# Attention and token mixing on one core: value products in three pieces, a plan that counts instructions, and the queries' factor on another engine

## The chip, the cores and the metric

One NeuronCore of a Trainium2 chip. It has TensorE (matmuls, PE), VectorE (DVE), ScalarE (ACT), GpSimd (POOL) and SyncE (SP, which issues transfers here), each with a queue of its own that runs in order. The time is that of one execution on the device, in microseconds (us); lower is better.

## The reference

Thresholded attention over 8 batches x 8 heads, 576 rows, head size 64, and behind it a mixing layer over 512 channels, all in float32:

```
scores = (q @ k.T) / 8
attn = softmax over the scores >= max(scores) - tau, others 0
x = attn @ v                       # heads side by side: 576 x 512 for each batch
theta = x @ w_theta
y = w_tok_r @ (x * cos(theta)) + w_tok_i @ (x * sin(theta))
u = x + y
out = u + relu(u @ w_ch)
```

## The kernel before

Two heads make a pair; there are 32 pairs, four to a batch. A float32 factor is split into a high and a low part of a faster type (`q1, q2`, `k1, k2`, `xh, xl`, `zh, zl`, `wt_h, wt_l`), and a product is the sum of three products of parts.

A pair's attention is five *units* of 128 rows (`unit`, four with two heads, the last with the rest of both). For each: 12 or 6 score matmuls into banks 0 to 3 of PSUM (L572); a VectorE pass from PSUM with the factor -1/8 that also gives the row minimum (L587, factor in `gate`, a column of `small`); the exponential on ScalarE (L612); mask, multiply and row sum on VectorE (L619). The factor's sign follows tau's, and the maximum becomes a minimum by it.

The weights then have to be turned, keys onto partitions, into the tile `a`, of which there is one. Most pairs are turned by VectorE in blocks of 32 x 32 (L634, L636); for pairs 0 to 5 and every fourth one after, `BY_PE` is true and TensorE turns them (L652), with copies by ScalarE (L658, L670). The value product follows: for pairs turned by TensorE with 64 rows (L711), for the others with 32 rows and 64 columns (L688), `products` inside `values`, 18 groups of keys in one go into four banks (0 to 3) at once. Float32 matmuls are run in two passes each, so that 144 matmuls of the code are 288 in the trace. ScalarE copies the result into `xT` (L695, L698), and `divide` multiplies by the inverse row sums, turned by L739, stored and spread by transfers, on GpSimd or VectorE (L762).

The mixture of batch b (L814 for both channel products, L935 turns, L964 the token product) runs beside the attention of batch b + 1; the last one runs alone. At the start the weights w_theta and w_tok are split (`convert`) beside the first pairs.

The order on every engine is made ahead of time by a planner in the kernel. Every operation is given an engine, a duration, a key, what it reads and writes and the buffers it needs. `run` simulates the engines: of the operations that can begin about now it takes the one with the lowest key, for TensorE with an addition for a change of form (`SWITCH` in time, `favour` in the key). The order that comes out is the program; on the chip, semaphores alone decide when something begins. Keys are in units of which a pair has 9; the offsets and shares are the numbers of `AT`. Buffers more than one bank wide (scores and the L688 product) take banks 0 to 3 in the order of the code, which has the product of pair n - 1 behind units 0 and 1 of pair n (`vq`).

Of the kernel before, what the change touches and what calls it, by code (L numbers as in the profile page):

```python
# [28 lines left out]
PE, DVE, ACT, POOL, SP = range(5)  # L29

SEM = 0.06
TABLE = 1.29
AT = {
    "wait": 0.06, "margin": 0.0, "held": 1.155, "theta": 2.75, "theta_by": 2.91, "tok": 8.25, "tok_by": 4.06, "ch": 32.56,
    "ch_by": 6.81, "q": -4.55, "k": -10.96, "raw": -2.84, "v": -0.24, "m0": 8.14, "m1": 4.71, "score": -3.28, "nm": -0.39,
    "add": -2.31, "exp": -2.15, "mask": 0.59, "wrap": -0.41, "turn": 1.01, "copy": 2.31, "block": 0.3, "turn_by": 0.3,
    "last": 0.68, "v0": 6.08, "v1": 15.08, "vcopy": 7.63, "div": 3.45, "rows": -1.17, "dmul": -1.49, "x": -0.85, "x_by": 0.29,
    "wm": -8.18, "ev": 4.38, "zst": 1.58, "sin": 1.57, "zm": 2.24, "zh": 1.93, "zl": -4.81, "y": -5.29, "u": 1.65, "fa": -0.31,
    "fa_by": 1.34, "ft": 0.17, "ft_by": 0.15, "pq": 29, "px": 2, "pu": 1, "pz": 7, "pk": 1, "ta": 4, "cut": 2, "pp": 0,
    "vm": 0, "m6": -0.56, "wp": 0, "wq": 0, "ua": 4, "ord": 0, "hang": 0, "n_rawq": 2, "n_rawk": 1, "n_q": 4, "n_rb": 2,  # L40
    "n_ang": 2, "n_xh": 4, "n_xl": 4, "n_wm": 3, "n_z": 3, "n_k": 4, "n_s2": 3, "n_nm": 4, "n_sc": 4, "n_a": 1, "n_zh4": 4,
    "n_zl4": 4, "n_zh1": 2, "n_zl1": 2, "n_xT": 7, "n_v": 1, "n_rows": 2, "n_rt": 1, "keep": -1.73, "linger": 0.03,
    "v_r": -0.13, "v_m": 0.0, "t_s": -0.57, "m_s": 1.63, "wc": 14, "early": 6, "each": 1, "ka": 4, "vq": 1, "pd": 4,
# [67 lines left out]
class Op:  # L111

    def __init__(self, n, eng, occ, tail, fn, key, lock, mode):
        self.n, self.eng, self.occ, self.lat, self.fn, self.key = n, eng, occ, occ + tail, fn, key
        self.lock, self.mode = lock, mode
        self.deps, self.after, self.bufs = {}, [], []
        self.start, self.left, self.ready, self.kb, self.then = None, 0, 0.0, 0.0, None


class Plan:  # L120
# [4 lines left out]
    def op(self, eng, occ, fn, key, R=(), W=(), tail=0.07, lock=False, mode=None, hold=()):  # L125
        o = Op(len(self.ops), eng, occ, tail, fn, key, lock, mode)
        o.hold = hold

        def need(d, full):
            if d is not o:  # L130
                o.deps[d] = o.deps.get(d, False) or full

        for x in R:
            b, parts = x if isinstance(x, tuple) else (x, list(x.writers))
            for p in parts if isinstance(parts, list) else [parts]:
                for d in b.writers.get(p, ()):
                    need(d, True)
                if b.psum:
                    for d in b.readers.get(p, ()):
                        need(d, d.eng != eng)  # L140
                b.readers.setdefault(p, []).append(o)
            if b not in o.bufs:
                o.bufs.append(b)
        for x in W:
            b, parts = x if isinstance(x, tuple) else (x, 0)
            for p in parts if isinstance(parts, list) else [parts]:
                for d in b.writers.get(p, []) + b.readers.get(p, []):
                    need(d, d.eng != eng)
                b.writers[p], b.readers[p] = [o], []
            if b not in o.bufs:  # L150
                o.bufs.append(b)
        for b in o.bufs:
            b.left += 1
        for d in o.deps:
            d.after.append(o)
        o.left = len(o.deps)
        self.ops.append(o)
        return o

    def run(self):  # L160
# [9 lines left out]

        def begin(o):
            t = max(free[o.eng], o.ready)
            taken = {}
# [49 lines left out]
        while todo:  # L223
# [48 lines left out]
def tile_attn_moe(  # L272
# [89 lines left out]
    def c_pool(n):  # L362
        return n * 0.0024 + 0.066

    def pe(occ, fn, key, R, W, mode="m", hold=()):
        return op(PE, occ, fn, key, R, W, tail={"m": 0.21, "t": 0.22, "v": 0.28, "w": 0.28, "r": 0.28}[mode], mode=mode, hold=hold)
# [30 lines left out]
    def convert(src, n, raw_cls, places, key, done, turn):  # L397
# [34 lines left out]
        if turn < AT["wc"]:  # L432
            for i in range(2):
                gps(
                    c_pool(n // 2), lambda i=i: clamp(nc.gpsimd, slice(n * i // 2, n * (i + 1) // 2)), key, ((mag, i),),
                    ((mag, i),),
                )
        else:
            dve(c_fast(n), lambda: clamp(nc.vector), key, (mag,), ((mag, [0, 1]),), lock=True)
# [33 lines left out]
        for c in range(0, n, n2):  # L473
# [9 lines left out]
            pe(0.485 * n2 / 288 + 2 * c_mm(n2), sum_up, key, (bits, w, hi_b), (ps,))  # L483
# [40 lines left out]
    def prepare_q(n, key):  # L524
# [3 lines left out]
        q1, q2 = pr.q = [sb("q", [P, QS], F32R) for _ in range(2)]  # L528
        act(c_act(QS), lambda: nc.scalar.copy(out=q1(), in_=raw()), key, (raw,), (q1,))  # L529
# [25 lines left out]
    def unit(n, i):  # L555
# [11 lines left out]
        def score():  # L567
# [11 lines left out]
            mode="r" if i < 4 else "m",  # L579
# [3 lines left out]
        for j in heads:  # L583
            sc = scs[j] = sb("sc", [P, S])
            dve(
                c_ps(S) + 0.008,
                lambda j=j, sc=sc: nc.vector.tensor_scalar(  # L587
                    out=sc().rearrange("p (a b) -> p a b", a=2), in0=ps()[:, 2 * j : 2 * j + 2, :HS], scalar1=gate, scalar2=None,
# [6 lines left out]
            0.1,  # L595
# [32 lines left out]
        if not pe_way:  # L628
            for j in heads:
# [8 lines left out]
                dve(c_two(S), blocks, t0 + j + AT["block"], ((s, j),), ((a, (i, j)),), lock=True)  # L638
# [6 lines left out]
        for x, (c0, nb) in enumerate(runs):  # L645
# [8 lines left out]
            pe(0.109 * nb, turn_round, t0 + AT["turn"] + AT["turn_by"] * x, ((s, list(heads)),), (tp,), mode="t", hold=(a,))  # L654
# [8 lines left out]
            else:  # L663
# [10 lines left out]
                act(2 * halves * c_act(nb * 64, True), lay, t0 + AT["copy"] + AT["turn_by"] * x, (tp,), ((a, (i, x)),))  # L674

    def values(n, key):
        pr, x = pairs[n], xT[n]
        a, v = pr.a, pr.v
        if not BY_PE(n):
# [3 lines left out]
            def products():  # L683
                for c in range(18):
# [7 lines left out]
            pe(18 * w / 600 + 0.05, products, key, (a, v), (ps,), mode="w", hold=[x])  # L692
# [22 lines left out]
        pe(9 * w / 600 + 0.05, products, key, (a, v), outs, mode="v", hold=[x])  # L715
# [10 lines left out]
    def divide(n, key):  # L726
# [13 lines left out]
            mode="t", hold=(rt,),  # L740
        )
        act(c_act(P, True), lambda: nc.scalar.copy(out=rt(), in_=tp()[:9, :P]), key + AT["rows"], (tp,), (rt,))
# [38 lines left out]
    def mixture(b, k0, k1):  # L781
# [11 lines left out]
        def product(which, m, parts, last_chunk, evict, hold=()):  # L793
# [10 lines left out]
            for run in runs:  # L804
                for q in range(0, len(run), 4 if len(run) % 4 == 0 else 3):
# [6 lines left out]
                    def go(piece=piece, h=h, first=first, final=final):  # L812
# [9 lines left out]
                        (ps[h],), hold=hold,  # L822
# [4 lines left out]
        def angle(m):  # L827
# [42 lines left out]
            )  # L870
            dve(
# [53 lines left out]
        def flip(m, keys):  # L925
            z = zs[m]
            out = []
            for (c0, nb), key in zip(((0, 4), (4, 1), (5, 4)), keys):
# [11 lines left out]
                pe(0.109 * nb, turn, key, ((z, zp(0) if c0 == 0 else zp(0, 1) if c0 == 4 else zp(1)),), (tp,), mode="t", hold=(zh, zl))  # L940
# [11 lines left out]
        def token(m):  # L952
            zz = zs[m, "T"]
            for h in range(2):
# [4 lines left out]
                for q in range(0, len(work), 3):  # L959
# [13 lines left out]
                    pe(3 * c_mm(HS), go, now(0.393), (*need.values(), *ws), (ps,))  # L973
# [153 lines left out]
```

## Time and profile before

| | us |
|---|---|
| three runs | 998.86, 999.94, 1008.34 |
| median | 999.94 |
| profiled execution, its time | 997.56 |
| its span in the profile | 995.8 |

The profile is one execution; its busy times, waits and timelines are read against its own 997.56 us. A line such as `L688` is a line of the kernel before. PE are matmuls and PEld the weight loads that overlap them.

### The profile page before, as it was taken

The page shows a single profiled execution, that of the slowest core. Times are in us where ns is not written, and L with a number is a line of the kernel's source. Part 1 is how long each engine was busy: PE and PEld are TensorE (multiplying, and loading weights), DVE is VectorE, ACT ScalarE, POOL GpSimd, SP SyncE. Part 2 cuts the span into 40 slices and gives each one's busy share as a digit, 9 for nine tenths or more (in the row PEclk, how much of TensorE's full clock was granted, in tenths as well). Part 3 has the DMA queues.
Part 4 walks back from the last instruction along what each step waited for, and adds up shares of the span by engine and source line. Part 5 has one row for each costly group of instructions (what it writes and reads, how often), then busy time and mean ns, then how long its engine had stood idle before and what let it go on. Part 6 is the DMA issues. An engine that isn't in the chain of part 4 may idle for free.

```text
span 995.8 us, 29743 instructions
## 1 busy us (share of the span) xinstructions
PE 917.0 (92%) x12357; PEld 808.2 (81%) x12357; DVE 822.6 (83%) x1963; ACT 606.6 (61%) x1154; POOL 337.8 (34%) x380
## 2 busy tenths in 40 slices
PE   6888899999899998999999998999999998998998
PEld 4565687888798877888888887898788887988898
DVE  7999968879799796997989797997979797986352
ACT  6888888546673556646675566646565466724550
POOL 4466354213351233512354143512344133500200
PEclk9999999999999999999999999999999999999999
DMA  6673234425433464225633365135633354222502
GB/s 229 196 209 110 62 125 132 145 82 167 154 82 80 124 192 111 68 58 161 183 83 75 97 185 169 46 81 150 182 85 84 96 155 142 59 51 74 176 19 69
DMA packets 59863, 118.21 MB, mean 119 GB/s; under 512 B 20272, under 2 KB 29008, under 8 KB 57296
## 3 DMA queue, kind: packets, MB, share of 16 engines
q1 hardware_dynamic: 59728, 116.31, 40.3%
q8 instruction: 97, 1.59, 0.7%
q14 instruction: 38, 0.31, 0.1%
HBM read 102.50 MB, written 13.78 MB: 117 GB/s over the span
## 4 chain that ended last, share of the span: by engine, by line
PE 52%; DVE 26%; issue 8%; ACT 7%; POOL 5%; DMA 1%; SPq 0%; DVEq 0%; POOLq 0%; ACTq 0%
PE banks_ps__66 L964 18%; PE banks_ps__66 L688 10%; PE banks_ps__66 L814 9%; DVE s L619 8%; DVE sc L587 8%; PE banks_ps__66 L572 8%; DVE a L634 3%; PE banks_ps__66 L935 3%; PE banks_ps__66 L652 2%; POOL z L910 2%; ACT s L612 2%; PE banks_ps__66 L711 1%; POOL q L385 1%; POOL xl L385 1%; ACT a L670 1%
## 5 line engine op out<-in xcount | busy, mean ns | idle before, releaser
L612 ACT ACTIVATE s<-sc,nm 128x576 f32<-128x576 f32 x288 | 218.4, 777 | 182.6 <-DVE sc L587 180.9
L619 DVE SCALAR_TENSOR_TENSOR s<-sc,nm,s 128x576 f32<-128x576 f32 x288 | 249.5, 893 | 17.9 <-ACT s L612 12.5
L587 DVE TENSOR_SCALAR_CACHE_REDUCE sc<-banks_ps__66,small 128x576 f32<-128x576 f32 x288 | 224.8, 800 | 18.2 <-PE banks_ps__66 L572 18.2
L572 PE MATMUL banks_ps__66<-k,q 64*128 64x288 f32 (+1 forms) x1728 | 176.7, 314 | 15.1 <-ACT q L529 6.5
L814 PE MATMUL banks_ps__66<-xh,wm 128*128 128x288 f32 x1024 | 173.5, 305 | 2.4 <-ACT xh L775 2.3
L572 PEld LDWEIGHTS banks_ps__66<-k,q 64*128 64x128 f32 (+1 forms) x1728 | 138.8, 189 | 42.7 <-DVE sc L587 13.3
L964 PE MATMUL banks_ps__66<-wt_h,zh 128*128 128x288 f32 x576 | 160.8, 303 | 3.4 <-DVE zl L944 2.2
L964 PE MATMUL banks_ps__66<-wt_l,zh 128*128 128x288 f32 x576 | 157.4, 297 | 0.0
L814 PEld LDWEIGHTS banks_ps__66<-xh,wm 128*128 128x128 f32 x1024 | 145.6, 190 | 11.6 <-ACT xh L775 5.1
L634 DVE STREAM_TRANSPOSE a<-s 128x576 f32<-128x576 f32 x152 | 111.7, 760 | 41.8 <-PE banks_ps__66 L688 41.5
L762 POOL TENSOR_TENSOR xT<-xT,rb 128x288 f32<-128x288 f32 x64 | 52.7, 840 | 240.9 <-ACT xT L695 153.0
L385 POOL TENSOR_TENSOR k<-rawk,k 128x288 fp32r<-128x288 f32 x64 | 57.0, 910 | 221.9 <-ACT k L537 191.6
L688 PE MATMUL banks_ps__66<-a,v 32*64 32x144 f32 x5472 | 98.2, 285 | 26.6 <-issue 26.5
L910 POOL TENSOR_TENSOR z<-z,xT 128x288 f32<-128x288 f32 x112 | 94.5, 874 | 79.6 <-ACT z L891 79.6
L688 PEld LDWEIGHTS banks_ps__66<-a,v 32*64 32x64 f32 x5472 | 87.1, 130 | 35.8 <-issue 33.1
L964 PEld LDWEIGHTS banks_ps__66<-wt_h,zh 128*128 128x128 f32 x576 | 108.9, 189 | 6.4 <-issue 3.1
L964 PEld LDWEIGHTS banks_ps__66<-wt_l,zh 128*128 128x128 f32 x576 | 108.7, 189 | 1.2 <-issue 1.2
L964 PE MATMUL banks_ps__66<-wt_h,zl 128*128 128x288 f32 x576 | 93.8, 300 | 0.0
L814 PE MATMUL banks_ps__66<-xl,wm 128*128 128x288 f32 x512 | 92.9, 300 | 0.0
L652 PE MATMUL banks_ps__66<-ident,s 128*128 128x128 f32 (+1 forms) x533 | 79.0, 285 | 9.3 <-DVE s L619 7.9
L964 PEld LDWEIGHTS banks_ps__66<-wt_h,zl 128*128 128x128 f32 x576 | 81.0, 188 | 1.2 <-issue 1.1
L652 PEld LDWEIGHTS banks_ps__66<-ident,s 128*128 128x128 f32 (+1 forms) x533 | 60.2, 143 | 22.0 <-DVE s L619 10.5
(76 smaller groups left out, 1267.4 us busy)
## 6 DMA issues: line engine op xcount, KB each, us to landing
wm<-wm_dram SPq DMA_DIRECT2D x64, 512.0 KB
v<-in_vp_dram SPq DMA_DIRECT2D x102, 288.0 KB
rawq<-in_qT_dram SPq DMA_DIRECT2D x32, 320.0 KB
rawk<-in_kT_dram SPq DMA_DIRECT2D x32, 288.0 KB
out_dram<-xT SPq DMA_DIRECT2D x31, 288.0 KB
rb<-sums_dram SPq DMA_DIRECT2D x64, 128.0 KB
z<-in_w_tok_dram SPq DMA_DIRECT2D x9, 576.0 KB
wm_dram<-rb SPq DMA_DIRECT2D x16, 256.0 KB
```

Source lines behind the costliest of these rows:

```text
L385: eng.tensor_tensor(out=out()[:, c0:c1], in0=in0()[:, c0:c1], in1=in1()[:, c0:c1], op=ALU.subtract)
L572: nc.tensor.matmul(ps()[:, 2 * j + h, :HS], q[a]()[r, i * P : (i + 1) * P], k[c]()[r, h * HS : (h + 1) * HS], start=(x == 0), stop=(x == 2),)
L587: lambda j=j, sc=sc: nc.vector.tensor_scalar(out=sc().rearrange("p (a b) -> p a b", a=2), in0=ps()[:, 2 * j : 2 * j + 2, :HS], scalar1=gat ...
L612: lambda j=j, sc=sc, weights=weights: nc.scalar.activation(out=weights(), in_=keys(sc()), func=AF.Exp, bias=nm()[:, j : j + 1], scale=-1.0),
L619: lambda j=j, sc=sc, total=total, weights=weights: nc.vector.scalar_tensor_tensor(out=weights(), in0=keys(sc()), scalar=nm()[:, 2 + j : 3 ...
L634: nc.vector.transpose(out=a()[:, :, j, 32 * i : 32 * i + 32], in_=src.rearrange("p (c q) -> p c q", q=32))
L652: nc.tensor.transpose(out=tp()[: k1 - k0, c * P : (c + 1) * P], in_=flat()[:, k0:k1], identity=ident)
L688: nc.tensor.matmul(ps()[64 * h : 64 * h + 64, b, :w], v()[r, c, h, :], a()[r, c, h, :], start=(c == 0), stop=(c == 17))
L762: eng.tensor_tensor(out=x()[:, r], in0=x()[:, r], in1=rc()[:, r], op=ALU.mult)
L814: nc.tensor.matmul(ps[h]()[:, :HS], wm()[:, a, c, :], parts[c][bb]()[:, h * HS : (h + 1) * HS], start=first and n == 0, stop=final and n = ...
L910: eng.tensor_tensor(out=zi, in0=zi, in1=x[m]()[:, c0:c1], op=ALU.mult)
L964: nc.tensor.matmul(ps()[:, :HS], zz[c][lo]()[:, zz[c][2]], w[:, c, hs], start=(q + n == 0), stop=(q + n == len(work) - 1),)
```

## The change

1. The product of a VectorE-turned pair (L688) is three operations of the plan, with six of the 18 key groups each, keys `vs` = 8.05 units apart, starting at `v1` = 3.55 (before: one, at 15.08). They add to the same four banks.
2. Every TensorE operation tells its number of instructions. `supply` models a queue that is filled in blocks of 256, the next one ready 3.6 us after a block is begun, and lengthens TensorE operations by what they starve; a piece of an L688 product counts as beginning only so much later when the next operation is picked.
3. From pair 2 on (`sq`) ScalarE multiplies the raw queries by `gate`, in place, before they are cast, and L587 multiplies by the immediate 1.0 in place of the pointer to `gate`.
4. One more pair, pair 5, is turned by VectorE (`early` 6 to 5).
5. Shares: two of four `u` remainders on GpSimd instead of one (`pu`); the division of every fourth pair on VectorE, the rest on GpSimd (`pd` 4 to 3); the cast of the fourth `u` on VectorE (`ua` 4 to 3); the q remainder on GpSimd from pair 4, not 3 (`pq`).
6. Some durations of the plan are changed (L587, L596, L634, the clamps on GpSimd times 1.7, two copies), and all keys and waits of `AT` are new. `ab` is 0, so its new branch is not used. No number of buffers (`n_...`) is changed.

```diff
+BLOCK = 256
+FETCH = 3.6
...
-    "v_r": -0.13, "v_m": 0.0, "t_s": -0.57, "m_s": 1.63, "wc": 14, "early": 6, "each": 1, "ka": 4, "vq": 1, "pd": 4,
...
+    "linger": 0.174, "v_r": 1.74, "v_m": -2.19, "t_s": 1.07, "m_s": -9.19, "wc": 14, "early": 5, "each": 1, "ka": 4, "vq": 1,
+    "pd": 3, "vs": 8.05, "parts": 3, "ab": 0, "sq": 2,
...
+        block = [80, 0.0]
+
+        def supply(o, t, occ):
+            left, (at, ready), x = o.count, block, t
+            while at + left >= BLOCK:
+                x, left, at = max(x + (BLOCK - at) * occ / o.count, ready), left - BLOCK + at, 0
+                ready = x + FETCH
+            return x + left * occ / max(o.count, 1) - t - occ, [at + left, ready]
+
         def begin(o):
             t = max(free[o.eng], o.ready)
+            if o.mode == "w":
+                t += supply(o, t, o.occ)[0]
...
                 occ += SWITCH(mode, o.mode)
                 mode = o.mode
+                starved, block = supply(o, t, occ)
+                occ += starved
...
         q1, q2 = pr.q = [sb("q", [P, QS], F32R) for _ in range(2)]
+        if n >= AT["sq"]:
+            act(
+                c_act(QS, ptr=True), lambda: nc.scalar.activation(out=raw(), in_=raw(), func=AF.Copy, scale=gate), key,
+                (raw,), (raw,),
+            )
...
             dve(
-                c_ps(S) + 0.008,
+                c_ps(S) + (0.0 if scaled else 0.06),
...
-                    out=sc().rearrange("p (a b) -> p a b", a=2), in0=ps()[:, 2 * j : 2 * j + 2, :HS], scalar1=gate, scalar2=None,
+                    out=sc().rearrange("p (a b) -> p a b", a=2), in0=ps()[:, 2 * j : 2 * j + 2, :HS], scalar1=1.0 if scaled else gate, scalar2=None,
...
-            def products():
-                for c in range(18):
+            def products(c0, c1):
+                for c in range(c0, c1):
                     for b in range(4):
                         r = slice(32 * b, 32 * b + 32)
                         for h in range(2):
                             nc.tensor.matmul(
                                 ps()[64 * h : 64 * h + 64, b, :w], v()[r, c, h, :], a()[r, c, h, :], start=(c == 0), stop=(c == 17)
                             )
 
-            pe(18 * w / 600 + 0.05, products, key, (a, v), (ps,), mode="w", hold=[x])
+            parts = AT["parts"]
+            for i in range(parts):
+                c0, c1 = 18 * i // parts, 18 * (i + 1) // parts
+                pe(
+                    (c1 - c0) * w / 600 + 0.05, lambda c0=c0, c1=c1: products(c0, c1), key + AT["vs"] * i, (a, v), (ps,),
+                    32 * (c1 - c0), mode="w", hold=[x],
+                )
```

## Rows read from the trace of the kernel before

**Rows 1.** The page's busy times: us, share of the span, instructions.

```profile
span 995.8 us, 29743 instructions
PE 917.0 (92%) x12357; PEld 808.2 (81%) x12357; DVE 822.6 (83%) x1963; ACT 606.6 (61%) x1154; POOL 337.8 (34%) x380
```

**Rows 2.** Busy time by stage: length, engines (instructions), TensorE's clock, DMA, GB/s.

```profile
0.00:100.00 100.00, 79.22 (x651) 58.16 (x651) 91.70 (x216) 78.00 (x163) 54.62 (x52) 0.97 0.61 185
100.00:213.00 113.00, 106.66 (x1063) 89.40 (x1065) 95.97 (x226) 84.18 (x172) 41.00 (x46) 1.00 0.36 111
...
556.00:670.00 114.00, 106.88 (x1651) 95.94 (x1652) 99.61 (x243) 67.97 (x126) 39.56 (x46) 1.00 0.43 118
```

**Rows 3.** TensorE's waits, whole run: total us, times, longest us.

```profile
PE banks_ps__66 L688 <- issue: 26.5, 22, 1.9
PE banks_ps__66 L739 <- DVE xT L1012: 9.3, 6, 1.6
```

**Rows 4.** The chain that ended last, 551 to 680 us: start, us, what.

```profile
611.08 1.32 issue
...
642.52 1.90 issue
```

**Rows 5.** The page's DMA queues, instruction blocks: packets, MB, share of engines.

```profile
q8 instruction: 97, 1.59, 0.7%
```

**Rows 6.** TensorE's timeline, three places: start, us, instructions merged.

```profile
571.68 1.20 PE L652 MATMUL banks_ps__66<-ident,s 128*128 128x128 f32 x9
...
607.30 0.69 PE L814 MATMUL banks_ps__66<-xh,wm 128*128 128x288 f32 x4
607.91 3.16 PE L688 MATMUL banks_ps__66<-a,v 32*64 32x144 f32 x183
...
612.40 1.96 PE L688 MATMUL banks_ps__66<-a,v 32*64 32x144 f32 x105 [1.32 <-issue]
614.29 0.66 PE L935 MATMUL banks_ps__66<-ident,z 128*128 128x128 f32 x4
```

**Rows 7.** VectorE's timeline, 607 to 622 us; in brackets the idle time before.

```profile
614.41 1.44 DVE L634 STREAM_TRANSPOSE a<-s 128x576 f32<-128x576 f32 x2 [5.20 <-PE banks_ps__66 L688]
...
618.59 0.69 DVE L944 TENSOR_TENSOR zl<-banks_ps__66,zh 128x512 fp32r<-128x512 f32 x1
619.20 0.81 DVE L587 TENSOR_SCALAR_CACHE_REDUCE sc<-banks_ps__66,small 128x576 f32<-128x576 f32 x1
...
619.93 0.76 DVE L866 SCALAR_TENSOR_TENSOR z<-ang 128x576 f32<-128x576 f32 x1
620.60 0.23 DVE L596 TENSOR_SCALAR nm<-nm,small 128x2 f32<-128x2 f32 x1
620.73 0.46 DVE L873 TENSOR_SCALAR z<-z 128x576 uint32<-128x576 uint32 x1
621.10 0.82 DVE L619 SCALAR_TENSOR_TENSOR s<-sc,nm,s 128x576 f32<-128x576 f32 x1
```

**Rows 8.** Waits: the first of the whole run, the others of 556:670.

```profile
DVE a L634 <- PE banks_ps__66 L688: 41.5, 12, 8.4
...
DVE a L634 <- PE banks_ps__66 L688: 6.5, 2, 5.2
...
PE banks_ps__66 L688 <- issue: 4.0, 3, 1.9
```

**Rows 9.** VectorE's timeline, 672 to 679 us, around a later product.

```profile
676.99 0.85 DVE L1012 SCALAR_TENSOR_TENSOR xT<-banks_ps__66,xT 128x288 f32<-128x288 f32 x2 [4.60 <-PE banks_ps__66 L814]
```

**Rows 10.** Groups by line and shape: count, busy us, mean ns, idle before.

```profile
L612 ACT ACTIVATE s<-sc,nm 128x576 f32<-128x576 f32 x288 | 218.4, 777 | 182.6 <-DVE sc L587 180.9
...
L688 PE MATMUL banks_ps__66<-a,v 32*64 32x144 f32 x5472 | 98.2, 285 | 26.6 <-issue 26.5
...
L529 ACT CAST q<-rawq 128x640 fp32r<-128x640 f32 x32 | 23.5, 733 | 0.2 <-DMA rawq<-in_qT_dram 0.2
...
L537 ACT CAST k<-rawk 128x576 fp32r<-128x576 f32 x32 | 21.8, 682 | 8.2 <-DMA rawk<-in_kT_dram 4.3 <-PE banks_ps__66 L572 3.7
```

More of the change, by code (lines that the diff above doesn't have):

```diff
@@ L33 @@
 AT = {
[L34 to L42, printed above, removed]
-    "v_r": -0.13, "v_m": 0.0, "t_s": -0.57, "m_s": 1.63, "wc": 14, "early": 6, "each": 1, "ka": 4, "vq": 1, "pd": 4,
+    "wait": 0.095, "margin": 46.124, "held": 12.206, "theta": 2.0, "theta_by": 8.31, "tok": 13.85, "tok_by": 3.19, "ch": 37.95,
+    "ch_by": 9.28, "q": -2.78, "k": -4.2, "raw": 1.32, "v": 5.53, "m0": 8.11, "m1": 8.41, "score": -169.95, "nm": -1.15,
+    "add": 0.82, "exp": -1.46, "mask": 2.68, "wrap": -18.89, "turn": 4.88, "copy": 2.04, "block": -0.74, "turn_by": -34.35,
+    "last": 6.86, "v0": 2.89, "v1": 3.55, "vcopy": 9.91, "div": -3.88, "rows": 6.2, "dmul": 15.26, "x": -12.78, "x_by": 4.06,
[3 rows of a table added]
+    "n_rb": 2, "n_ang": 2, "n_xh": 4, "n_xl": 4, "n_wm": 3, "n_z": 3, "n_k": 4, "n_s2": 3, "n_nm": 4, "n_sc": 4, "n_a": 1,
+    "n_zh4": 4, "n_zl4": 4, "n_zh1": 2, "n_zl1": 2, "n_xT": 7, "n_v": 1, "n_rows": 2, "n_rt": 1, "keep": -144.9,
+    "linger": 0.174, "v_r": 1.74, "v_m": -2.19, "t_s": 1.07, "m_s": -9.19, "wc": 14, "early": 5, "each": 1, "ka": 4, "vq": 1,
+    "pd": 3, "vs": 8.05, "parts": 3, "ab": 0, "sq": 2,
 }
@@ L363, in c_pool, with pe @@
         return n * 0.0024 + 0.066
-    def pe(occ, fn, key, R, W, mode="m", hold=()):
-        return op(PE, occ, fn, key, R, W, tail={"m": 0.21, "t": 0.22, "v": 0.28, "w": 0.28, "r": 0.28}[mode], mode=mode, hold=hold)
+    def pe(occ, fn, key, R, W, count, mode="m", hold=()):
+        tail = {"m": 0.21, "t": 0.22, "v": 0.28, "w": 0.28, "r": 0.28}[mode]
+        return op(PE, occ, fn, key, R, W, tail=tail, mode=mode, hold=hold, count=count)
     def act(occ, fn, key, R, W, hold=()):
@@ L636, in blocks @@
                         nc.vector.transpose(out=a()[:, :, :, P:], in_=src.rearrange("p (c h q) -> p c h q", h=2, q=16))
-                dve(c_two(S), blocks, t0 + j + AT["block"], ((s, j),), ((a, (i, j)),), lock=True)
+                dve(c_two(S) + 0.014, blocks, t0 + j + AT["block"], ((s, j),), ((a, (i, j)),), lock=True)
             return
@@ L713, in products @@
                         )
-        pe(9 * w / 600 + 0.05, products, key, (a, v), outs, mode="v", hold=[x])
+        pe(9 * w / 600 + 0.05, products, key, (a, v), outs, 144, mode="v", hold=[x])
         for par, o in enumerate(outs):
@@ L739, in divide @@
             0.06, lambda: nc.tensor.transpose(out=tp()[:9, :P], in_=rows()[:, :9], identity=ident), key, (rows,), (tp,),
-            mode="t", hold=(rt,),
+            2, mode="t", hold=(rt,),
         )
-        act(c_act(P, True), lambda: nc.scalar.copy(out=rt(), in_=tp()[:9, :P]), key + AT["rows"], (tp,), (rt,))
+        act(c_act(P, True) + 0.1, lambda: nc.scalar.copy(out=rt(), in_=tp()[:9, :P]), key + AT["rows"], (tp,), (rt,))
         load(lambda: nc.sync.dma_start(sums_dram[n], rt()), key + AT["keep"], (rt,), (kept,), 5)
@@ L821, in product @@
                         len(piece) * c_mm(HS), go, now(0.131 * len(piece)), (wm, *need.values()),
-                        (ps[h],), hold=hold,
+                        (ps[h],), 2 * len(piece), hold=hold,
                     )
@@ L870, in angle @@
             )
+            if m < AT["ab"]:
+                act(
+                    c_act(S), lambda: nc.scalar.activation(out=z()[:, :S], in_=z()[:, S:], func=AF.Abs), now() + AT["zst"],
+                    ((z, zp(1)),), ((z, zp(0)),),
+                )
+                return
             dve(
```

27 lines of the change are left out of this document (14 added, 13 removed), and 3 rows, old and new, of the table AT.

## The prediction

> **What bounds the kernel now.** I read the page's busy shares first, then busy time by stage, TensorE's waits, the chain through one batch, and the timelines of TensorE and VectorE around a value product.
>
> The busy shares name two engines: TensorE 92% and VectorE 83% of a span of 995.8 us [rows 1]. By stage they change places. In the first 100 us VectorE is busy 91.70 and TensorE 79.22; from then on TensorE is busy about 107 of 113 us, VectorE 96 to 100, and ScalarE 68 of 114 once the weights are converted [rows 2]. The granted clock is 1.00 there, so the clock explains nothing.
>
> TensorE's waits say what it lacks. The largest, 26.5 us in 22 pieces of at most 1.9 us, is "issue" at L688, the value products of the VectorE-turned pairs; next is 9.3 us at L739 [rows 3]. "Issue" means that no semaphore, buffer or engine held it. The chain and the timeline show the place: a product runs 183 matmuls, stands 1.32 us, and runs 105 more; the next one stands 1.90 us [rows 4, 6]. The stop is inside one accumulation and at another matmul each time, so neither data nor a bank is the cause. What fits is the supply of instructions: 97 instruction packets [rows 5] for 2 x 12357 TensorE instructions [rows 1] are 255 each, and a product has 288 matmuls (5472 over 19 pairs [rows 10]) and as many loads, 576 instructions, in about 4.6 us (below): 255 of them last 2.0 us. Elsewhere a matmul and its load take some 0.13 us, 255 instructions last 16 us, and no such stop is listed. If a block takes about 2.0 + 1.7 = 3.7 us to come, a product outruns it once, at times twice: 22 stops in 19 products.
>
> VectorE is the second engine to watch. Its 32-row transposes (L634) write the tile `a`, of which there is one, so they wait for the product that reads it: once for 5.20 us [rows 7], 6.5 us in this batch [rows 8]. During a later product it stands 4.60 us at L1012, whose L814 matmuls TensorE has queued behind the product [rows 9]. So some 11 of VectorE's 14.4 idle us of a batch (114 less 99.61 [rows 2]) lie in product windows.
>
> **The change, part by part.** *Three pieces.* Each product becomes three of 96 matmuls, 192 instructions each, fewer than a block, with other work between. If the other work lasts as long as a stop, the stop falls into it. Lower bound of the gain 0 (the pieces land back to back), upper bound 26.5 us [rows 3]. I take 24: a piece's 192 instructions last 1.5 us, and one mixture piece of 3 or 4 matmuls between (0.4 to 0.5 us) is too little, four are enough; the plan's model now holds a piece back while it would starve.
>
> Against it stand the changes of tile form. The last L814 matmul before a product starts near 607.30 + 3 x 0.13 = 607.69, the product at 607.91 [rows 6]: 0.22 instead of 0.13, so 0.09 going in. The last L688 matmul starts near 612.40 + 1.96 - 0.28 = 614.08, the next transpose at 614.29 [rows 6]: 0.21 instead of 0.016 (105 matmuls in 1.96), so 0.20 coming out. Two more round trips are 2 x 0.29 = 0.58 us for each product; 288 x 0.016 gives the 4.6 us used above. With 20 products (next edit) that is 11.6 us; the kernel's own table of switches (0.144 and 0.153 to 0.197) gives 12 to 14, so the upper bound is 14.
>
> *One more VectorE-turned pair* (pair 5; `early` 6 to 5). TensorE loses 41 transposes (nine blocks for each of four units, five for the last): nine L652 in a row start about 0.11 us apart (1.20 less a last 0.28, over 8 [rows 6]), so 4.5 us; the two forms of product cost about the same. VectorE gains nine transposes, about 0.68 apart (two in 1.44, each 0.76 long [rows 7]): 6.2 us, in a stage where it has 113 - 95.97 = 17 us free [rows 2]. I take -4; the bounds are -4.5 and 0 (if VectorE sets that stage after all).
>
> *Queries' factor on ScalarE.* From pair 2 on a 640-column ACTIVATE with a pointer scale comes ahead of the cast. Nearest rows: the cast of 640 columns takes 733 ns; at 576 columns an ACTIVATE with a pointer takes 777 and a cast 682 [rows 10]. So about 0.83 us, 30 times: 25 us of ScalarE, under 1 us per 28 us pair, hidden beside its 39% idle [rows 1]. It delays GpSimd's q part by as much; q is made a pair ahead with four buffers. If that lead were gone it would cost at most 25 us; I take 0.
>
> In return L587 loses its pointer scalar. L587 takes 0.73 us to the next start (619.20 to 619.93); a plain read of 512 columns of PSUM takes 0.61 (618.59 to 619.20), so 0.68 for 576 [rows 7]. 0.05 us are over, for pointer and accumulator together. A two-column pointer op (L596) takes 0.13, while 576 columns at double speed without a pointer (L873) take 0.37, of which 0.30 are columns [rows 7]: that speaks for the pointer. So 0 to 0.05 us, 270 times: 0 to 13.5 us of VectorE, 2 us a batch at most. In a stage bound by TensorE that is worth nothing by itself; in the first 100 us it is 18 instructions, 1 us. I take -1.
>
> *Shifted shares.* One `u` remainder per batch goes to GpSimd (`pu`), every fourth pair's division to VectorE (`pd`), one `u` cast to VectorE (`ua`), one q remainder to VectorE (`pq`): on VectorE about -0.7, +0.7, +0.4 us a batch, and +1 once. Sum near nothing; GpSimd at 34% covers its part. The new keys and corrected durations reorder everything; the product's last piece has a key 16 units behind its first, so pieces may stand far apart. What that does is bounded below; I take 0.
>
> *Sum.* 997.6 (the profiled execution's time: 995.8 and 1.8 around it) - 24 + 11.6 - 4 - 1 = 980.2. The runs' median, 999.9, lies 2.4 above the profiled execution, so **982** against it.
>
> The Trainium skill, "Runtime: NRT & Kernel Launch", section "Instruction fetch mechanics", has instructions arriving in blocks of 256, the next block fetched while one runs, and calls the cost of crossing "mostly hidden". The block agrees with 255 per packet; that it is hidden does not agree with the 26.5 us at L688. Taken at its word, the gain term would be 0 and the sum 1004.
>
> **The rivals.**
>
> *More than the stalls (0.14).* TensorE has some 15 us of smaller waits, and an order made with better durations may close part of them, with VectorE relieved by up to 2 us a batch. For it: L739's 9.3 us [rows 3]. Against: TensorE is full already. Half of 15 and VectorE's first stage: about 968.
>
> *Wait for wait (0.18).* The pieces hold banks 0 to 3 and `a` longer, scores of units 2 to 4 and the transposes start later, and VectorE's wait takes what TensorE gained. For it: the idle windows of rows 7 to 9. Time: about 997, the gain of 17 gone.
>
> *Slower: the held tile makes VectorE the bound (0.11).* VectorE's demand in a batch is 99.6 busy + 6.5 waiting for the product - 2 = 104; TensorE's new batch is 114 - 4.0 (three stops [rows 8]) + 1.7 = 112. So 8 us a batch, 2.6 us per product, are free: a product window may grow from 6.45 us (607.91 to 612.40 + 1.96 [rows 6]) to about 9. Beyond, each microsecond of window costs 20 us over 20 products, unless VectorE has the next pair's first two units (eight L587 and L619, 6 us) left to do in it. Windows of 11 us without that work would give 980 + 40 = 1020. Against it: these two units' scores go ahead of the product in the queue of banks, so the work can be there.
>
> *The stop is not the supply, or does not go away (0.07).* If stops come at each block whatever stands between, or come from this form of matmul, nothing is won and the switches stay: 997.6 + 11.6 - 4 = 1005, 1007 against the median. For it: no row shows a fetch itself. Against: one stop, at a wandering place, in 576 instructions, and none where instructions are used slowly. This is the case of the page's rule.
>
> **How the numbers follow.** The forecast (0.50) has its own range from the bounds: 26.5 to 18 us of stall removed, 14 to 11.6 paid, pair 5 between 4.5 and 0: 970 to 990. Faster by over 1% (about what a measurement here can tell from no change) is below 990: 0.50 + 0.14 = 0.64. Within 1% is *wait for wait* and most of the last rival: 0.18 + 0.04 = 0.22. Slower: 0.11 + 0.03 = 0.14. The range must reach from the larger gain to beyond *wait for wait*: 960 to 1005.
>
> **What would show it.** Right: "issue" at L688 falls from 26.5 us to a few; L688's matmuls come in runs of 96 (some 60 runs) with L814, L964 or L935 between; 20 pairs; TensorE's total of other waits is unchanged; the batch period drops by about 2 us. For the factor: L587's step to the next start falls from 0.73 towards 0.68, and ScalarE's busy time rises by 25 us less what pair 5's copies out of PSUM took. Wrong: VectorE's wait for L688 (41.5 us in the whole run [rows 8]) doubles and windows between first and last piece exceed 9 us: then the held tile is the price. Issue time that stays at 20 us or more means the supply was misread. If the issue time goes and the span does not, the step that failed is that TensorE alone sets the batch.

## The result and the profile after

The median fell from 1003.57 us (four runs of before beside it, 998.86 to 1008.34) to **966.56 us** (four runs, 965.98 to 967.92); the ratio is 0.9633, with a 95% interval of 0.9575 to 0.9691. The forecast was 982, with a range of 960 to 1005: the direction and the range held, and the point was 15 us too high. The gain was forecast at 18 us (999.9 less 982); it is 37.0 between these medians and 31.2 between the spans of the profiled executions. In the listing of after, the product L688 is L711, the 64-row product L711 is L740, the scores L572 and their pass L587 are L594 and L610, the transposes L634 are L657, the mixture's L814, L964 and L935 are L843, L999 and L970, and the additions L976 and L1012 are L1011 and L1047. The mask L619 is L642, the turns L652 are L675, the turns of row sums L739 are L768 (behind a VectorE step, L764), and `zh` and `zl` (L941, L944) are L976 and L979. L551 casts the queries, and L548 is the new ScalarE pass.

The page's first lines, to be read against [rows 1]:

```profile
span 964.6 us, 30108 instructions
PE 914.9 (95%) x12532; PEld 804.4 (83%) x12532; DVE 816.2 (85%) x1981; ACT 612.4 (63%) x1156; POOL 353.4 (37%) x378
```

Busy time by stage, against [rows 2]; the last line is one batch, as 556 to 670 us was in before:

```profile
0.00:100.00 100.00, 81.01 (x679) 60.71 (x680) 90.92 (x228) 83.96 (x174) 49.12 (x48) 1.00 0.61 192
100.00:213.00 113.00, 108.60 (x1391) 93.25 (x1391) 100.31 (x233) 80.41 (x158) 47.63 (x49) 1.00 0.40 116
540.00:650.00 110.00, 107.30 (x1592) 94.95 (x1597) 97.81 (x241) 68.85 (x125) 42.85 (x46) 1.00 0.43 122
```

TensorE is busy for about as long in all (914.9 against 917.0 us); it is idle time that went. In a batch it is busy 107.30 of 110.00 us where it was busy 106.88 of 114.00. TensorE's waits over the whole run (total, times, longest), against [rows 3]:

```profile
PE banks_ps__66 L594 <- DVE sc L610: 10.2, 16, 1.3
PE banks_ps__66 L768 <- DVE rows L764: 6.9, 11, 0.7
PE banks_ps__66 L594 <- ACT q L551: 6.4, 1, 6.4
PE banks_ps__66 L675 <- DVE s L642: 6.0, 9, 1.4
PE banks_ps__66 L711 <- issue: 5.5, 8, 1.4
```

"Issue" at the product is 5.5 us where it was 26.5. VectorE's waits, against [rows 8]:

```profile
DVE xT L1047 <- PE banks_ps__66 L843: 37.3, 17, 5.8
DVE zl L979 <- ACT zh L976: 33.3, 14, 3.6
DVE sc L610 <- PE banks_ps__66 L594: 20.9, 12, 5.4
DVE xT L1011 <- PE banks_ps__66 L999: 13.9, 9, 3.1
DVE a L657 <- PE banks_ps__66 L711: 11.2, 7, 2.8
```

The wait of the transposes for the product, which was to double if the held tile were the price, fell from 41.5 to 11.2 us. TensorE's timeline shows a product in its three pieces, against [rows 6]:

```profile
580.66 1.78 PE L711 MATMUL banks_ps__66<-a,v 32*64 32x144 f32 x96
582.37 0.79 PE L843 MATMUL banks_ps__66<-xh,wm 128*128 128x288 f32 x4
583.09 1.98 PE L711 MATMUL banks_ps__66<-a,v 32*64 32x144 f32 x96
585.00 0.79 PE L843 MATMUL banks_ps__66<-xh,wm 128*128 128x288 f32 x4
...
588.71 1.78 PE L711 MATMUL banks_ps__66<-a,v 32*64 32x144 f32 x96
590.42 0.79 PE L843 MATMUL banks_ps__66<-xh,wm 128*128 128x288 f32 x4
```

Each piece here runs its 96 matmuls through, and only 2.43 us pass from the first start to the second, with four matmuls of the mixture between.

**Where the 31.2 us of span were saved.** The products of three TensorE-turned pairs (4, 7 and 31) serve as marks. In before:

```profile
136.50 1.69 PE L711 MATMUL banks_ps__66<-a,v 64*64 64x288 f32 x24
...
238.06 4.60 PE L711 MATMUL banks_ps__66<-a,v 64*64 64x288 f32 x72
...
926.56 1.69 PE L711 MATMUL banks_ps__66<-a,v 64*64 64x288 f32 x24
```

and in after:

```profile
134.85 1.44 PE L740 MATMUL banks_ps__66<-a,v 64*64 64x288 f32 x20
...
224.81 1.44 PE L740 MATMUL banks_ps__66<-a,v 64*64 64x288 f32 x20
...
888.79 1.44 PE L740 MATMUL banks_ps__66<-a,v 64*64 64x288 f32 x20
```

The start gave 1.7 us, pairs 4 to 7 gave 11.6 (101.56 less 89.96), the 24 pairs from 7 to 31 gave 24.5 (688.50 less 663.98), which is 4.1 a batch where about 2 was expected, and the end took back 6.6 (69.24 to 75.81), since more of the mixture was left when the attention ended: behind the start of pair 31's product, 236 matmuls of L843 where before had 192 of L814.

### The profile page after: what moved, and what is told of

It reads as the page before. It is cut to its first block, busy times and chain, and to the rows that moved or that the text cites. A ratio compares the mean times of both kernels' runs of the same rounds, so it can differ in the third digit from the quotient of the medians.

```text
span 964.6 us, 30108 instructions
## 1 busy us (share of the span) xinstructions
PE 914.9 (95%) x12532; PEld 804.4 (83%) x12532; DVE 816.2 (85%) x1981; ACT 612.4 (63%) x1156; POOL 353.4 (37%) x378
## 4 chain that ended last, share of the span: by engine, by line
PE 52%; DVE 34%; ACT 7%; issue 4%; DMA 1%; POOL 1%; SPq 0%; DVEq 0%; ACTq 0%
PE banks_ps__66 L999 14%; PE banks_ps__66 L843 10%; PE banks_ps__66 L711 9%; DVE s L642 8%; DVE sc L610 8%; PE banks_ps__66 L594 8%; DVE a L657 6%; PE banks_ps__66 L675 4%; PE banks_ps__66 L740 3%; DVE zl L979 2%; DVE nm L619 1%; PE banks_ps__66 L970 1%; ACT s L635 1%; DVE z L895 1%; DVE xl L402 1%
## 5 line engine op out<-in xcount | busy, mean ns | idle before, releaser
L642 DVE SCALAR_TENSOR_TENSOR s<-sc,nm,s 128x576 f32<-128x576 f32 x288 | 255.1, 900 | 7.2 <-ACT s L635 5.3
L610 DVE TENSOR_SCALAR_CACHE_REDUCE sc<-banks_ps__66 128x576 f32<-128x576 f32 x270 | 195.6, 739 | 18.1 <-PE banks_ps__66 L594 17.9
L594 PE MATMUL banks_ps__66<-k,q 64*128 64x288 f32 (+1 forms) x1728 | 176.8, 312 | 19.1 <-DVE sc L610 10.2
L594 PEld LDWEIGHTS banks_ps__66<-k,q 64*128 64x128 f32 (+1 forms) x1728 | 138.6, 188 | 48.1 <-DVE sc L610 19.5
L843 PE MATMUL banks_ps__66<-xh,wm 128*128 128x288 f32 x1024 | 173.2, 303 | 0.4 <-ACT xh L804 0.4
L999 PE MATMUL banks_ps__66<-wt_h,zh 128*128 128x288 f32 x576 | 159.5, 300 | 1.1 <-DVE zl L979 1.1
L999 PE MATMUL banks_ps__66<-wt_l,zh 128*128 128x288 f32 x576 | 159.8, 300 | 0.0
L843 PEld LDWEIGHTS banks_ps__66<-xh,wm 128*128 128x128 f32 x1024 | 143.8, 188 | 11.6 <-issue 9.2
L657 DVE STREAM_TRANSPOSE a<-s 128x576 f32<-128x576 f32 x160 | 116.4, 756 | 14.5 <-PE banks_ps__66 L711 11.2
L791 POOL TENSOR_TENSOR xT<-xT,rb 128x288 f32<-128x288 f32 x48 | 38.4, 819 | 226.1 <-ACT xT L724 122.5
L711 PE MATMUL banks_ps__66<-a,v 32*64 32x144 f32 x5760 | 110.0, 287 | 5.5 <-issue 5.5
L999 PEld LDWEIGHTS banks_ps__66<-wt_h,zh 128*128 128x128 f32 x576 | 108.2, 188 | 4.4 <-issue 2.8
L999 PEld LDWEIGHTS banks_ps__66<-wt_l,zh 128*128 128x128 f32 x576 | 108.2, 188 | 4.0 <-issue 3.7
L711 PEld LDWEIGHTS banks_ps__66<-a,v 32*64 32x64 f32 x5760 | 91.8, 130 | 17.9 <-issue 17.1
L402 POOL TENSOR_TENSOR k<-rawk,k 128x288 fp32r<-128x288 f32 x64 | 64.7, 1031 | 107.2 <-ACT k L559 70.3
L999 PE MATMUL banks_ps__66<-wt_h,zl 128*128 128x288 f32 x576 | 96.0, 301 | 0.0
L843 PE MATMUL banks_ps__66<-xl,wm 128*128 128x288 f32 x512 | 94.5, 301 | 0.0
L402 POOL TENSOR_TENSOR xl<-xT,xh 128x288 fp32r<-128x288 f32 x64 | 62.5, 1003 | 71.5 <-ACT xh L804 70.1
L999 PEld LDWEIGHTS banks_ps__66<-wt_h,zl 128*128 128x128 f32 x576 | 81.0, 188 | 5.1 <-issue 5.0
L979 DVE TENSOR_TENSOR zl<-banks_ps__66,zh 128x512 fp32r<-128x512 f32 (+1 forms) x96 | 50.0, 544 | 34.0 <-ACT zh L976 33.3
```

Of the source, the lines that this page charges most:

```text
L402: eng.tensor_tensor(out=out()[:, c0:c1], in0=in0()[:, c0:c1], in1=in1()[:, c0:c1], op=ALU.subtract)
L594: nc.tensor.matmul(ps()[:, 2 * j + h, :HS], q[a]()[r, i * P : (i + 1) * P], k[c]()[r, h * HS : (h + 1) * HS], start=(x == 0), stop=(x == 2),)
L610: lambda j=j, sc=sc, scaled=scaled: nc.vector.tensor_scalar(out=sc().rearrange("p (a b) -> p a b", a=2), in0=ps()[:, 2 * j : 2 * j + 2, :H ...
L642: lambda j=j, sc=sc, total=total, weights=weights: nc.vector.scalar_tensor_tensor(out=weights(), in0=keys(sc()), scalar=nm()[:, 2 + j : 3 ...
L657: nc.vector.transpose(out=a()[:, :, j, 32 * i : 32 * i + 32], in_=src.rearrange("p (c q) -> p c q", q=32))
L711: nc.tensor.matmul(ps()[64 * h : 64 * h + 64, b, :w], v()[r, c, h, :], a()[r, c, h, :], start=(c == 0), stop=(c == 17))
```

## The experiments

Times are medians of four executions, of ten for before_pieces. Each ratio is to before on the same chip, whose medians there were 1001.30 to 1003.86 us; after itself was timed in a group of its own, so small differences from it are read from the ratios. The columns "stands" and "other" are sums over the trace of one execution, of steps from one matmul's start to the next: "stands" are steps of over 0.1 us inside a product, "other" are all steps of over 0.25 us that aren't inside one.

| kernel | us | ratio to before (95%) | stands | other |
|---|---|---|---|---|
| before | 1003.57 | 1 | 38.0 | 106.8 |
| after | 966.56 | 0.9633 (0.9575 to 0.9691) | 17.7 | 85.9 |
| after_one_go | 1013.12 | 1.0112 (1.0074 to 1.0149) | 46.4 | 110.7 |
| after_pointer | 980.81 | 0.9774 (0.9751 to 0.9796) | 16.1 | 103.0 |
| before_immediate | 992.70 | 0.9902 (0.9871 to 0.9934) | 40.5 | 94.8 |
| before_pieces | 1009.65 | 1.0064 (1.0037 to 1.0092) | 23.1 | 129.3 |
| after_one_go_late | 1026.32 | 1.0214 (1.0164 to 1.0264) | 41.7 | 131.2 |
| after_immediate | 967.66 | 0.9637 (0.9603 to 0.9672) | 16.7 | 87.0 |
| after_pair5_tensore | 984.05 | 0.9803 (0.9769 to 0.9837) | 16.3 | 100.3 |
| after_plan_uncounted | 1015.29 | 1.0109 (1.0072 to 1.0147) | 38.1 | 120.1 |
| after_two_runs | 971.24 | 0.9676 (0.9621 to 0.9732) | 24.5 | 92.4 |
| after_plan_shifted | 973.76 | 0.9710 (0.9662 to 0.9759) | 16.5 | 94.2 |
| after_old_durations | 1016.33 | 1.0131 (1.0080 to 1.0181) | 22.7 | 136.9 |

**A long run: what makes the stops.** Pair 13's first piece is repeated until 960 matmuls of this form stand in a row (one execution).

```diff
-                for c in range(c0, c1):
+                for x, c in enumerate([*range(c0, c1)] * (10 if n == 13 and c0 == 0 else 1)):
```

> The kernel after, but pair 13's first piece repeats its six groups ten times in one go (960 matmuls, 1920 instructions; that pair's values come out wrong). Supply theory: about 2.0 us of work for each 255 instructions, then a stop of about 1.7 us, at a distance of 128 matmuls each time: six or seven stops, the run 15.4 + 11 = about 26 us. If the stop comes from the start of a product or from its operands, one stop at most and about 16 us. Clock: if stops of 1.7 us lower the granted clock, it is 0.5 for part of this stretch and the pace of matmuls there doubles.

It took 985.85 us, and the 960 matmuls 27.3, where 26 were expected. TensorE's timeline in the run:

```profile
392.32 2.44 PE L711 MATMUL banks_ps__66<-a,v 32*64 32x144 f32 x136
395.51 2.27 PE L711 MATMUL banks_ps__66<-a,v 32*64 32x144 f32 x128 [0.74 <-issue]
399.51 2.27 PE L711 MATMUL banks_ps__66<-a,v 32*64 32x144 f32 x128 [1.74 <-issue]
...
411.24 2.27 PE L711 MATMUL banks_ps__66<-a,v 32*64 32x144 f32 x128 [1.46 <-issue]
414.97 2.27 PE L711 MATMUL banks_ps__66<-a,v 32*64 32x144 f32 x128 [1.46 <-issue]
418.42 1.22 PE L711 MATMUL banks_ps__66<-a,v 32*64 32x144 f32 x56 [1.19 <-issue]
```

The stop comes at every 128th matmul, which with its load is every 256th instruction, and a block comes every 4.00 us, later every 3.73 us (399.51 to 403.51, 411.24 to 414.97), while 128 matmuls use it up in some 2.3. No engine, bank or data changes at that number. The trace holds the transfers of instructions too. From 395.5 to 418.4 us, where six blocks begin, the DMA view has

```profile
q8 instruction: 6, 0.10, 2.1%
```

which is one packet of 16,384 bytes for each block. The packets start at 396.97, 400.61, 404.62, 408.64, 412.34 and 416.09 us, 1.1 to 1.5 us after a block begins, and the next block's first matmul comes 2.3 to 2.9 us behind that. So the supply of instructions is shown to be the cause, the fetch for which the prediction had no row can be seen, and it isn't semaphores alone that decide when something begins. The Trainium skill, "Runtime: NRT & Kernel Launch", section "Instruction fetch mechanics", has blocks of 256, which agrees; that crossing into the next is "mostly hidden" does not hold for this form, at up to 1.74 us a block. The part of the expectation that failed is the clock (below).

**Pieces in one go, in the order of after.** On TensorE pieces 2 and 3 are moved right behind piece 1; the order of every other engine stays.

```diff
+            first, *rest = o.pieces
+            for r in rest:
+                line.remove(r)
+            k = line.index(first)
+            line[k + 1 : k + 1] = rest
```

> The kernel after, with its own order on every engine, but on TensorE the second and third piece of each product stand right behind the first. Theory 1 (supply: the pieces are worth the stops they avoid, less their switches): issue time at the products comes back to about 20 to 28 us, 40 round trips of 0.29 us fall away, so 967 + 20 - 11.6 = about 975. Rival (the pieces hold the tile and banks 0 to 3 for 8 to 10 us, and that is a price): releasing them 2 to 3 us earlier per product gives more back than the stops cost, 966 or less.

It took 1013.12 us, 46.6 more than after. TensorE's first wait, and VectorE's two (L754 is the product, L1057 the addition L1011 of after, L1025 its L979):

```profile
PE banks_ps__66 L754 <- issue: 32.5, 25, 2.3
...
DVE xT L1057 <- PE banks_ps__66 L1045: 65.9, 18, 7.0
DVE zl L1025 <- ACT zh L1022: 52.8, 15, 7.8
```

The stops are back, at 28.7 us by the count (46.4 less 17.7), and 39 round trips of form fewer, at 0.29, give back 11.3. The other steps take 24.8 more (110.7 less 85.9), and with these the count comes to 42.2 of the 44.8 us between first and last matmul (954.5 and 999.3). They go with waits between engines: VectorE stands, in its fixed order, before additions whose matmuls were to run between the pieces (13.9 to 65.9 us). So the loss is not the price of the stops alone, and the opposite move was tried:

```diff
+            *rest, last = o.pieces
...
+            k = line.index(last)
+            line[k:k] = rest
```

> The kernel after, own order on every engine, but the first and second piece of each product wait until the third and run right before it: one go again, with the mixture work that stood between the pieces ahead of it and so no later than in the kernel after. Theory 1 (stops against switches): 20 us of stops come back, 11.4 us of switches go, about 976. Theory 2 (after_one_go lost its 46 us because it puts that mixture work 3 to 5 us later, and VectorE stands in order waiting for it): about 976 here too, far below after_one_go's 1013, the rest being the later free tile. Rival (the one-go form itself costs 40 us in this order, by stops and the low clock that follows them): near 1010.

It took 1026.32 us, not 976. Now the transposes (L700) wait for the late product, and the additions L1093 (L1047 of after) longer for their matmuls:

```profile
DVE a L700 <- PE banks_ps__66 L754: 53.5, 13, 5.6
DVE xT L1093 <- PE banks_ps__66 L889: 49.0, 17, 8.3
```

In an order made for pieces, one go costs on whichever side the pieces are gathered. What a new plan for one-go products, with the durations of after, would give wasn't tried. Moving only the second piece leaves two runs, of 192 and 96 matmuls:

```diff
+            first, *rest = o.pieces
+            line.remove(rest[0])
+            line.insert(line.index(first) + 1, rest[0])
```

> The kernel after, own order on every engine, but the second piece of each product stands right behind the first, the third stays where it is: 384 instructions, other work, 192. Supply theory: 384 instructions cross one block edge or two, and only the second within a run stands, so about half the products stop: issue time about 15 us, 20 round trips of switches less (5.7 us). With the price of work put later as in after_one_go, about half of its 46 us: 985 to 992. If the time jumps to 1010 already, it is not the stops but the first gap that counts; if it stays under 972, the second gap is what counts.

```profile
PE banks_ps__66 L752 <- issue: 12.2, 14, 1.8
```

It took 971.24 us. Its interval overlaps that of after, so the 4.7 us are not told from nothing; the gap ahead of the last piece does most of the work.

**Pieces in the order of before.** The product of before is cut in three, with up to three small mixture operations drawn into each gap where some could begin (six gaps stay empty); the order of the other engines stays.

```diff
+                    new[k : k + 1] = [(o, f[0], False), *gaps[0], (o, f[1], False), *gaps[1], (o, f[2], True)]
```

> The kernel before, all other engines in their old order; on TensorE each product is cut in three, with the one or two small pieces of work that followed it (0.4 to 0.9 us each gap) put between. Theory 1 (supply): a part of the stops, 10 to 18 of 26.5 us, is filled, 11 us of switches are paid: 0 to 7 us faster. Rival (held tile): products end 1 to 2 us later, VectorE waits, 5 to 20 us slower. If the stops do not shrink, the supply theory is wrong.

It took 1009.65 us, 6.8 more than before beside it (1002.90). TensorE's issue wait and VectorE's two largest (L748 is the product, L694 the transposes, L647 the score pass):

```profile
PE banks_ps__66 L748 <- issue: 9.3, 14, 1.9
...
DVE a L694 <- PE banks_ps__66 L748: 50.1, 12, 8.9
DVE sc L647 <- PE banks_ps__66 L632: 43.6, 18, 7.5
```

Issue falls from 26.5 to 9.3 us with nothing changed but the cut and the work drawn into the gaps; 32 more round trips cost 9.3, and the other steps grow by 22.5 (106.8 to 129.3). The profiled execution is one of the slower of the ten (1012.50 us), so these sums overstate the loss. Here *wait for wait* is what happened: in this order the cut does not pay.

**The factor.** In after, L610 gets its pointer back, to a column of ones, and nothing else changes:

```diff
-... scalar1=1.0 if scaled else gate, ...
+... scalar1=unit_col if scaled else gate, ...
```

> The kernel after, same order on every engine, but the score pass L610 reads its factor 1.0 through a pointer to a column again (the queries are still scaled ahead). Each of the 270 passes gets 0.07 us longer (739 against 810 ns), 19 us of VectorE. Theory 1 (TensorE alone sets the steady batches): at most 3 us slower, 967 to 970. Rival (VectorE sets part of the time, so its relief was part of the gain that the forecast lacked): 8 to 15 us slower, 975 to 982.

It took 980.81 us, 14.2 more than after. In before, the pointer is taken away (`scalar1=-1.0 / root`):

> The kernel before, same order, but L587 multiplies by the immediate -0.125 in all 288 passes, with nothing added on ScalarE (the sign for a negative tau is left out). Theory 1 (TensorE alone): 0 to 2 us faster. Rival (VectorE sets part of the time): 288 x 0.07 = 20 us less VectorE, of which 6 to 14 us show.

It took 992.70 us, 10 less than before. From one L587 or L610 to VectorE's next start it is 737 to 738 ns (median) with a pointer in both orders and 677 to 678 without: 0.061 us, 270 times, 16.5 us of VectorE. TensorE's waits of after_pointer, with L770 the turns of row sums and L596 the scores:

```profile
PE banks_ps__66 L770 <- DVE rows L766: 12.3, 12, 1.5
PE banks_ps__66 L596 <- DVE sc L612: 12.2, 17, 1.1
...
PE banks_ps__66 L713 <- issue: 4.8, 6, 1.4
```

Issue stays where it was (4.8 against 5.5), and it is TensorE's waits for VectorE that grow: 6.9 to 12.3 and 10.2 to 12.2, and 17.1 us over all other steps (85.9 to 103.0). TensorE does not set the steady batches alone. Whether ScalarE pays for it is seen by leaving its pass out:

```diff
-... lambda: nc.scalar.activation(out=raw(), in_=raw(), func=AF.Copy, scale=gate), key,
+... lambda: None, key,
...
-... scalar1=1.0 if scaled else gate, ...
+... scalar1=-1.0 / root if scaled else gate, ...
```

> The kernel after, same order, without the 30 multiplications of the queries on ScalarE; L610 multiplies by the immediate -0.125 instead (the sign for a negative tau is left out). It takes 25 us off ScalarE and 0.8 us off the way of each pair's queries. If ScalarE is cover, as the prediction had it: 0 to 1.5 us faster. Rival (ScalarE's pass delays the exponentials in its queue, which VectorE waits for): 4 to 12 us faster.

967.66 us, the same as after: the 24.7 us of the L548 pass (30 times 825 ns, forecast 0.83 us) are hidden.

```profile
L548 ACT ACTIVATE rawq<-rawq,small 128x640 f32<-128x640 f32 x30 | 24.7, 825 | 0.9 <-DMA rawq<-in_qT_dram 0.9
```

**The plan.** In the next four kernels one input of the planner is changed and the order is made anew with the keys of after. Its supply model returns nothing (`return 0.0, block`):

> The kernel after with three pieces and the same keys, but a plan that does not count instructions (no starving in the model), planned anew. If the gaps come from the keys alone: issue time at the products 6 to 12 us, time within 5 us of 967. If the count is what places the gaps: pieces land closer (11 of 20 products have two pieces back to back or nearly), issue time over 12 us, 975 to 985.

```profile
PE banks_ps__66 L712 <- issue: 17.4, 22, 1.7
...
DVE sc L611 <- PE banks_ps__66 L595: 49.4, 21, 7.7
```

1015.29 us: pieces alone do not keep the stops away. Without the count they land closer together: 11 of the 40 gaps hold no other matmul, where after has one such gap. The start of the first block is put elsewhere (`block = [208, 0.0]` for 80), half a block (128 instructions) further on:

> The kernel after, planned anew with the model's instruction count set off by half a block (208 for 80), nothing else changed. If the gaps work because the plan knows where the block edges are: stops come back, issue time over 12 us, 980 or more. If it only matters that pieces are under a block and stand apart: issue time 4 to 8 us, and what the time changes by is what any new order costs with keys not searched for it: 967 to 985, which then also bounds what the 17 us of after_pair5_tensore say of pair 5.

973.76 us with as few stops (16.5 against 17.7): the phase does not matter for them. The 7 us, whose interval overlaps that of after, are what one order cost for which the keys weren't fitted, if they are anything. The changed durations are put back, of which these are four:

```diff
-                c_ps(S) + (0.0 if scaled else 0.06),
+                c_ps(S) + 0.008,
...
-            0.14,
+            0.1,
...
-                dve(c_two(S) + 0.014, ...
+                dve(c_two(S), ...
...
-                    c_pool(n // 2) * 1.7, ...
+                    c_pool(n // 2), ...
```

> The kernel after, planned anew with the durations of before (L610, L619, L657, the clamps, two copies) and the same keys. If the corrected durations carry part of the gain: slower by more than after_plan_shifted, by 10 us or more, with VectorE's and TensorE's waits for each other up. If not: the same as after_plan_shifted within 5 us.

```profile
PE banks_ps__66 L594 <- DVE sc L610: 15.0, 24, 1.5
...
PE banks_ps__66 L711 <- issue: 6.7, 7, 1.4
...
DVE a L657 <- PE banks_ps__66 L711: 38.6, 8, 7.4
```

1016.33 us, 50 more than after, with issue still at 6.7: it is waits between engines that come back (other steps 85.9 to 136.9). That is seven times what the one unfitted order above cost, but keys fitted to these durations weren't tried, so the 50 us hold the durations and the misfit of the keys together. With pair 5 turned by TensorE again (`early` 6):

> The kernel after with pair 5 turned by TensorE again (early 6), planned anew by the same rules, so the order changes elsewhere too. By the prediction's step: +4 us, about 971. Rival (the stage of pairs 4 to 6 gained 11.6 us by this pair alone): +8 to +12.

984.05 us. The 17.5 hold pair 5 and the unfitted order (7 us at one sample) together and can't be parted. Of the 16.9 us between first and last matmul (954.5 and 971.4), 14.4 are longer other steps (85.9 to 100.3), so most of it is waits and not the 41 transposes.

## Why the prediction was right or wrong

**The stops: right.** The cause, the block of 256 and its period (3.7 forecast, 3.73 to 4.00 measured) stand. The gain was 21.0 us by the waits (26.5 less 5.5) and 20.3 by the count, where 24 was taken.

**The switches: right.** A step into a product is 0.22 us and out of it 0.21 by the median; 40 more round trips (59 against 19) at 0.29 are 11.6 us, as forecast.

**ScalarE at nothing: right**, by after_immediate. Its busy time rose by 5.8 us only (606.6 to 612.4), where 25 less pair 5's copies was named as a sign; a cast in each batch had gone to VectorE as well.

**The pointer: the term that was mis-sized.** Its duration lay just over the bounds (0.061 where 0 to 0.05 stood). What failed is the next sentence, "in a stage bound by TensorE that is worth nothing by itself". It was worth 14 us in the order of after and 10 in that of before, where 1 was taken. The prediction's own figures of a batch held the warning: TensorE 112 us of need, VectorE 104 with its waits. Two engines that feed each other in fixed orders, 8 us apart, did not leave the second one free here. Without this term the sum was -16.4 us; after_pointer, which lacks it too, has 17.1 us less than before from the first matmul to the last (985.6 to 968.5). So the pointer is nearly all of the 15 us by which the point missed. The agreement of 16.4 and 17.1 is partly luck: by the count, stops and switches of after_pointer make 10.3 (21.9 less 11.6), where 12.4 was forecast, and its other steps give 3.8, where nothing was; the 3.0 that remain are pair 5, taken at 4, and the clock together.

**Two sums of the prediction.** Its own range, 970 to 990, is not what its bounds add up to: with 26.5, 11.6, 4.5 and 1 the low end is 977 for the profiled execution, 980 against the median; with 18, 14 and nothing else the high end is 994. Only the pointer's upper bound of 13.5 us, which was named and left out, leads below 970. The 4.60 us that it counts among the idle time of the batch of 556 to 670 us lie at 672 to 677, in the next one; over all 19 products VectorE stood 3.60 us in each on average, some 10 a batch, so the reading holds roughly.

**The order at nothing: right only in sum.** The other steps of after_pointer are 103.0 us against 106.8 of before, so the new order won little there by itself. But it was no small thing: the same cut costs 6.8 us in the old order, and other plans of the same pieces cost 7 to 50.

**"The clock explains nothing": true only of the batch shown.** The cores' view of before and of after:

```profile
core 0: 995.8 us, clock 0.991
```

```profile
core 0: 964.6 us, clock 1.000
```

Before has five dips to 0.50 (1.2 of 2.4 GHz), three of them behind the first 100 us. At most 0.9% of its span, 9 us, was lost so, and up to 5 us of what lies between before and after_pointer (mean 0.996) may be the clock. The runs' own clocks say more. At 0.996 after took 966.74 and 967.92 us and after_pointer 979.79 to 981.16, so the pointer's price is 13 us at one clock; and before_immediate gained its 10 us at a mean of 0.986. The 27 executions of before beside the experiments had 0.976 to 0.992 and took 998.25 to 1008.94 us, the longer the lower the clock; a straight line through them loses 6.8 us for each 0.01 and would come to some 994 us at 1.000. That is an estimate, since none ran there; by it, some 9 of the 37 us between the medians are the clock and 28 are not. Whether the stops are what lowered it no run shows.

**The rivals.** *The stop is not the supply* falls by the long run. *The held tile* falls in after: a product's window, first matmul to end, grew from 6.57 to 8.97 us on average, just under the 9 named as free (8 of 20 are over it), but VectorE's idle time in it fell from 3.60 to 3.11. That the scores of the next pair give it work there is likely, and not shown apart. VectorE's wait for the product did grow in before_pieces (41.5 to 50.1 us, its window 6.57 to 7.26) and, where the product comes late, in after_one_go_late (53.5). *More than the stalls*, at 968, came nearest in time; its "VectorE relieved by up to 2 us a batch" is the pointer, and the smaller waits it hoped to close fell by 20.9 us (106.8 to 85.9) with that relief and by 3.8 without it.

**Left open:** what three pieces are worth against a one-go plan with keys and durations of its own, since after_one_go and before_pieces each change one engine's order under the others' old ones; pair 5 (4 forecast, bounded only by the 17.5); how much the durations carry with keys of their own; and what lowers the clock.

## What to carry to other kernels

Count instructions per microsecond wherever matmuls are tiny: here a block of 256 came every 3.7 to 4.0 us, so runs of this form longer than 128 matmuls stood, and two runs of 96 needed other work between them. When a second engine is within a tenth of the first, price its small per-instruction costs at up to their full sum, not at nothing, and test them alone by changing one operand. An edit to one engine's order in a program whose other orders are fixed can cost more than it saves; make the whole order anew, with measured durations, before the edit is judged.

## What the runs showed of the hardware that was not expected

The clock went down after some stands and not after others. In before, a stand of 1.58 us ended at 829.67 us, by TensorE's timeline,

```profile
829.67 0.28 PE L739 MATMUL banks_ps__66<-ident,rows 128*9 128x128 f32 x1 [1.58 <-DVE xT L1012]
```

and by the windows of 1 us the clock is 1.00 (2.4 GHz) there, and 0.50 (1.2 GHz) from 831 us on:

```profile
829.00:830.00 1.00, 0.33 (x2) 0.21 (x2) 1.00 (x4) 0.72 (x2) 0.00 (x0) 1.00 0.10 37
...
831.00:832.00 1.00, 1.00 (x8) 0.72 (x5) 1.00 (x4) 1.00 (x4) 0.00 (x0) 0.50 0.27 99
...
833.00:834.00 1.00, 1.00 (x6) 1.00 (x5) 1.00 (x3) 0.23 (x1) 0.00 (x0) 0.50 0.00 0
```

In the long run, stands of 0.74 to 1.74 us in each of seven blocks left it at 1.00:

```profile
400.00:404.00 4.00, 2.27 (x147) 2.00 (x130) 0.00 (x0) 0.00 (x0) 0.00 (x0) 1.00 0.04 6
```

The other two dips of before behind its first 100 us came 1.3 to 1.4 us after stands of 1.62 and 1.85 us. What makes the difference no run here shows. The second thing is the price of a pointer in a VectorE pass over 128 x 576 elements from PSUM: 0.061 us (738 against 677 ns to the next start) for an instruction that computes the same.
